# Output weights prepared from pair 48 on, first token rows ahead of the last transpose, and warming products on half the rows

## Chip, core and metric

The kernel runs on one core of one Trainium2 chip. The metric is the device time of one execution in microseconds (us). A core has TensorE (PE, the matrix engine; its weight loads are shown apart as PEld), VectorE (DVE), ScalarE (ACT), GpSimd (POOL) and SyncE (SP, which here issues nearly all DMAs). Each engine works through its own instructions in their order and waits for the others through semaphores. All DMAs that SP issues go through one queue to 16 DMA engines.

## The reference, cut to what matters

Two independent parts stand side by side in the output of 2048 x 1152.

Part A is attention with a compressive memory: 32 heads of 18, four segments of 512 tokens.

```python
q, k, v = x @ wq, x @ wk, x @ wv             # [2048, 576], 32 heads x 18
for s in range(4):                           # segments of 512 tokens
    p = softmax(q_s @ k_s.T * scale + causal mask)
    a_dot = p @ v_s
    a_mem = (phi(q_s) @ M) / (phi(q_s) @ z + 1e-6)
    o_s = g * a_mem + (1 - g) * a_dot
    M, z = M + phi(k_s).T @ v_s, z + sum(phi(k_s))
a = o @ wo                                   # the output product, [2048, 576]
```

Part B is a Fourier mixing by dense matrices: `y = Cr @ (x @ Hr.T) - Ci @ (x @ Hi.T)`, with Cr and Ci of 2048 x 2048 and Hr and Hi of 576 x 576.

## The kernel before

Products that need more than 16-bit accuracy are done with operands split in two, `hi` (rounded) and `lo` (the rest), as hi x lo + hi x hi + lo x hi. Rounding is done on ACT (`high`), the difference on DVE or POOL (`low`).

**Start.** `warm_up` (L237 to L239) issues products of a tile of ones while the first inputs are on their way; the tile of ones is set by DVE, nothing reads the result, and the first products of the projections (L250) follow on PE in its order. Projections, memory and lookups of the four segments fill the first 225 us or so.

**Pairs.** Attention then runs over 64 pairs of heads (a pair is two heads of a segment, one of them, `odd`, softmaxed row by row and then transposed by a DMA, the other, `even`, computed transposed at once). `attention()` is a software pipeline of 68 pairs `p`, each of eight slots; a slot is a stretch of recording that ends at a `yield`. Between slots the main loop records products of part B (`dense()`, L583, L628 to L633), as many as keep part B's planned cost in step with attention's. So the order of instructions on each engine is set when the program is recorded; it does not depend on times on the chip. Part B's left operands arrive in chunks (`craw`), four steps of a product to a chunk; ACT rounds them to `chi` (L451) and POOL, one tick later, makes `clo` (L456), two chunks ahead of their use. `later(n, ...)` puts a step n slots off.

**The tail of a pair's life.** In slot 5 `f_turn` asks SP for the transpose of the odd head's probabilities, from `hl` to `ptt` (L1003). `pv` (L1076, L1077) multiplies probabilities and values, `pv_out` normalises them, `turn_out` turns them and stores them to the DRAM buffers `od`.

**The output stage.** The output product works on token rows loaded back from `od`, two tiles of 128 tokens at a time (t and t + 8), by a scheme with seven products of half-size blocks instead of eight. It needs

- right operands: blocks of `wo` and sums and differences of them, each as hi and lo. `right_operands()` makes them; `load` fetches a row block of `wo` (`raw`), `first_block`, `second_row`, `tails`, `tail_difference` and `combined` round on ACT (`high`, L707), `difference` subtracts (L739), `block_low`, `row_low` and `combined_low` make low parts (`low`, L710) on POOL or DVE. Sums are written over `raw` in place. `combined` and `combined_low` write into the buffers of `qs0`/`ks0` to `qs2`/`ks2` when the last group of heads that uses them is done.
- left operands: `left(n)` is a generator of six steps that prepares tiles n and n + 8 from the rows `o_load` fetched. For n = 0 the rows go to `oraw` tiles in the buffers of `ks3`, `qs3`, `phi` and `plo`, and the results to those of `pf` and `hl`; for n = 0 all additions are on DVE, otherwise some are on POOL.

`PLAN` holds steps by slot: `at(p, slot, fn, ...)` runs `fn` right after that slot of pair p has been recorded. `right_operands` fills it. After the last pair the main loop records what is left of part B, with one step of `left(1)` for each piece, and then `output_stage()`, where `p1`, `p6`, `p5`, `p7`, `p2` follow each other for a tile pair; `p6` adds into `u` on DVE (L883), and `p7` writes the same PSUM tile next.

Before the change, the steps of `right_operands` stand at pairs 57 to 67: four `difference` and then four `combined_low` on DVE in pairs 64 and 65 for the first half, and eight more in pair 67 for the second, one after the other; rows 0 and 8 are asked for after slot 5 of pair 66, that is after the last transpose, rows 1 and 9 after slot 4 of pair 67, and all of `left(0)` is recorded at that place too.

Of the kernel before, what the change touches and what calls it, by code (L numbers as in the profile page):

```python
# [12 lines left out]
F32 = mybir.dt.float32  # L13
# [9 lines left out]
S, D, H, DH, NSEG, L = 2048, 576, 32, 18, 4, 512  # L23
P = 128
# [16 lines left out]
def infini_attention_and_fnet(ctx: ExitStack, tc: tile.TileContext, xT, wqk, w8, wv, wo, beta, xtT, cT, hT, out):  # L41
    nc = tc.nc
    act, dve, pool, pe = nc.scalar, nc.vector, nc.gpsimd, nc.tensor
# [23 lines left out]
    ones = const.tile([P, P], BF16, name="ones")  # L67
# [32 lines left out]
    ps = p1.enter_context(tc.tile_pool(name="ps1", bufs=2, space=PSUM))  # L100
# [43 lines left out]
    def wide_tile(cols):  # L144
        return lambda: wide.tile([P, cols], F32R, name="wide", tag="wide")
# [56 lines left out]
    for i in range(2):  # L202
        kn.append(tuple(sk.tile([P, D], F32R, name=f"kn{n}{i}") for n in "hl"))
        t = sk.tile([P, 2, H, 19], F32R, name=f"vn{i}")
# [3 lines left out]
    for i in range(3):  # L208
        t = sb.tile([P, H, 55], BF16, name=f"vs{i}")
# [25 lines left out]

    def warm_up():
        o = ps.tile([P, L], F32, name="warm", tag="acc", bufs=5)  # L237
        for _ in range(38):
            pe.matmul(o[:, :P], ones, ones, start=True, stop=True)  # L239

    def open_qk(s):
        ms = (0, 1, 2, 3) if s else (0, 1, 2, 3, 8)
        for m in ms:
            FIRST[m] = ps.tile([P, L], F32, name="qk", tag="acc", bufs=5)
        terms = {m: qk_terms(s, m) for m in ms}
        edges = (0, 6, 14) if s else (0, 1, 2, 3, 6, 9, 14)
        for a, b in zip(edges, edges[1:]):
            for m in ms:
                for n in range(a, b):
                    pe.matmul(FIRST[m], *terms[m][n], start=n == 0, stop=n == 13)  # L250
                if s and m == 0 and a:
                    accumulate(3, (1,))
            if s and a == 0:
                accumulate(3, (0,))
# [245 lines left out]
    for s in range(NSEG):  # L500
        more = s < 3
        if s == 0:
            warm_up()
# [55 lines left out]
    ps = ctx.enter_context(tc.tile_pool(name="ps2", bufs=2, space=PSUM, reuse_waits="tile"))  # L559
# [122 lines left out]
    O, LEFT, WO, TAIL = {}, {}, {}, {}  # L682
# [13 lines left out]
    def right_operands():  # L696
        raw, late = {}, {}

        def at(p, slot, fn, *a):
            PLAN.setdefault(8 * p + slot, []).append((fn, a))  # L700

        def load(k):
            raw[k] = wide.tile([P, D], F32, name="wide", tag="wide") if k == 3 else sb.tile([P, D], F32, name="raw", tag="raw", bufs=3)
            dma(raw[k], wo[k])

        def high(o, k, cs=slice(0, D)):
            act.activation(o, raw[k][:, cs], AF.Copy)  # L707

        def low(engine, o, hi, k, cs=slice(0, D), rows=slice(0, P)):
            engine.tensor_tensor(o[rows], raw[k][rows, cs], hi.bitcast(F32)[rows], OP.subtract)  # L710

        L_, R_ = slice(0, 288), slice(288, D)
        lower, upper = slice(0, 64), slice(64, P)

        def first_block(c):
            b = late["b", c] = wide.tile([P, 2, 288], F32R, name="wide", tag="wide")
            WO["B11", c] = b[:, 0], b[:, 1]
            high(b[:, 0], c, L_)

        def second_row(c):  # L720
            hi, lo = late["r", c] = [wide_tile(D)() for _ in range(2)]
            WO["B21", c], WO["B22", c] = ((hi[:, cs], lo[:, cs]) for cs in (L_, R_))
            high(hi, c + 2)

        def tails():
            w = late["w"] = [wide_tile(D)() for _ in range(2)]
            TAIL[1], TAIL[2] = ([t[:, cs] for t in w] for cs in (L_, R_))
            for t in w:
                high(t, 4)

        def tail_difference():
            d = wide.tile([P, 2, 288], F32R, name="wide", tag="wide")
            TAIL[0] = [d[:, i] for i in range(2)]
            for t in TAIL[0]:
                high(t, 4, L_)

        def difference(engine, o, a, b):
            (ko, co), (ka, ca), (kb, cb) = o, a, b
            engine.tensor_tensor(raw[ko][:, co], raw[ka][:, ca], raw[kb][:, cb], OP.subtract)  # L739

        def stage(i, n):
            return (sr if i < 2 else sq).tile([P, 4, 256], F32R, name="late", tag=f"{n}s{i}").rearrange("p a x -> p (a x)")

        def combined(c, n):
            k, names = ((c, ("T1", "T3")), (c + 2, ("T4", "T2")))[n]
            if c and n:
                hi, lo = ([t[:, D:D + 288] for t in late["s", i]] for i in (1, 0))
            else:
                late["s", 2 * c + n] = [stage(2 * c + n, x) for x in "qk"]
                hi, lo = ([t[:, L_], t[:, R_]] for t in late["s", 2 * c + n])  # L750
            for i, x in enumerate(names):
                WO[x, c] = hi[i], lo[i]
            if c and n:
                for i in range(2):
                    high(hi[i], k, (L_, R_)[i])
            else:
                high(late["s", 2 * c + n][0][:, :D], k)

        def combined_low(c, n, i):
            k, names = ((c, ("T1", "T3")), (c + 2, ("T4", "T2")))[n]  # L760
            low(dve, WO[names[i], c][1], WO[names[i], c][0], k, (L_, R_)[i])

        def block_low(c):
            low(pool, WO["B11", c][1], WO["B11", c][0], c, L_)

        def row_low(c):
            low(pool, late["r", c][1], late["r", c][0], c + 2)

        def sums(c):
            a, b = c, c + 2  # L770
            return (((a, L_), (a, R_), (a, L_)), ((a, R_), (b, R_), (a, R_)),
                    ((b, R_), (b, R_), (a, L_)), ((b, L_), (b, L_), (b, R_)))

        at(57, 2, load, 0)
        at(57, 4, load, 2)
        at(58, 2, first_block, 0)
        at(58, 2, second_row, 0)
        at(58, 2, load, 4)
        at(58, 4, load, 3)
        at(58, 4, block_low, 0)  # L780
        at(59, 4, row_low, 0)
        at(59, 2, tails)
        at(60, 4, lambda: low(pool, late["w"][0], late["w"][0], 4, rows=lower))
        at(61, 2, second_row, 1)
        at(61, 4, lambda: low(pool, late["w"][1], late["w"][1], 4, rows=upper))
        at(62, 4, difference, pool, (4, L_), (4, L_), (4, R_))
        at(63, 2, tail_difference)
        at(62, 6, row_low, 1)
        at(63, 4, lambda: low(pool, TAIL[0][0], TAIL[0][0], 4, L_, lower))
        at(63, 6, lambda: low(pool, TAIL[0][1], TAIL[0][1], 4, L_, upper))  # L790
        at(63, 6, load, 1)
        at(64, 2, first_block, 1)
        at(64, 4, block_low, 1)
        for i, x in enumerate(sums(0)):
            at(64, 3 + i, difference, dve, *x)
            at(65, 3 + i, combined_low, 0, i // 2, i % 2)
            at(67, 1, difference, dve, *sums(1)[i])
            at(67, 3, combined_low, 1, i // 2, i % 2)
        for n in range(2):
            at(65, 2, combined, 0, n)  # L800
            at(67, 2, combined, 1, n)
        for t in (0, 8):
            at(66, 5, o_load, t, lambda t=t: sq.tile([P, 4, 256], F32, name="oraw", tag="qs3" if t else "ks3").rearrange(
                "p a x -> p (a x)")[:, :5 * P].rearrange("p (k x) -> p k x", k=5))
        for t, tag in ((1, "phi"), (9, "plo")):
            at(67, 4, o_load, t, lambda tag=tag: sa.tile([P, 5, P], F32, name="oraw", tag=tag, bufs=2))
        at(67, 4, lambda: list(left(0)))

    def left(n):
        one, two = O.pop(n), O.pop(n + 8)  # L810
# [130 lines left out]
    sq = ctx.enter_context(tc.tile_pool(name="sb2q", bufs=1, side="right", reuse_waits="tile"))  # L941
    sa = ctx.enter_context(tc.tile_pool(name="sb2a", bufs=1, reuse_waits="tile"))
# [262 lines left out]
    while due:  # L1205
        tick()
    td = ta = 0.0
    right_operands()
    for n, w in enumerate(attention()):
        tick()  # L1210
# [3 lines left out]
        while td / total_d < ta / total_a:  # L1214
            t = next(d, BREAK)
# [5 lines left out]
    prepare = left(1)  # L1221
# [54 lines left out]
```

## Time and profile before

| | us |
|---|---|
| median of 3 runs | 993.38 (992.39 to 993.64) |
| profiled execution, time | 994.13 |
| profiled execution, span from first to last instruction | 992.4 |
| PE busy | 980.9 |
| DVE busy | 786.4 |
| ACT busy | 714.7 |
| POOL busy | 675.2 |

In the profile, times are in us unless marked ns. A row of a timeline gives start, duration, engine, line of the kernel, operation, output<-input with the program's names, shapes and count; what stands in brackets is the idle time before it and what ended it. SPq is SP's DMA queue issuing: its duration is that of the issue, not of the transfer. Matmuls are pipelined, so the duration of one is longer than its distance to the next. A row of windows gives from:to, its length, then for PE, PEld, DVE, ACT and POOL the busy time and number of instructions, the granted clock, the share of the DMA engines and the GB/s that they moved; where such a row is taken for the instructions of one line alone, it has only the engines that run that line.

### The profile page before, as it was taken

Reading aid. Unit: us, or ns where it says so; the run is one execution under the profiler, and the core shown is the slowest. Engines: PE = TensorE matmul, PEld = TensorE weight load, DVE = VectorE, ACT = ScalarE, POOL = GpSimd, SP = SyncE. Lnnn points to the kernel's source line nnn. Section 1 sums busy time; section 2 is a strip of 40 time slices with the busy share of each in tenths; the row PEclk is TensorE's granted clock in tenths of the full one; section 3 lists DMA queues with packets and bytes.
Section 4 is the critical chain, followed back from the end, with each engine's and each line's share of the span. In section 5 each row is a group of like instructions: output and inputs, shape, how many; then the busy total and the mean of one; then the engine's idle time right before and its main releaser. Section 6 shows DMA issues by size and latency. Waiting matters only on the chain.

```text
span 992.4 us, 25495 instructions
## 1 busy us (share of the span) xinstructions
PE 980.9 (99%) x9246; PEld 918.3 (93%) x9246; DVE 786.4 (79%) x2115; ACT 714.7 (72%) x1687; POOL 675.2 (68%) x744
## 2 busy tenths in 40 slices
PE   9999999999999999999999999999999999999998
PEld 8988989898999999999999999999999999999998
DVE  6657668584678787887898878888888898989985
ACT  6757576563888777877878788886777778788442
POOL 2657576686676667676775777767676667887561
PEclk9999999999999999999999999999999999999999
DMA  7537556777578898899999998779999999988663
GB/s 241 191 117 244 194 170 241 238 243 214 146 179 206 224 239 227 203 226 241 223 253 242 235 211 191 187 196 218 247 231 219 224 241 252 249 200 180 168 199 112
DMA packets 304351, 209.97 MB, mean 212 GB/s; under 512 B 204992, under 2 KB 259136, under 8 KB 304192
## 3 DMA queue, kind: packets, MB, share of 16 engines
q1 hardware_dynamic: 304000, 208.20, 80.9%
q8 instruction: 72, 1.18, 0.5%
q14 instruction: 55, 0.45, 0.1%
q10 hardware_dynamic: 224, 0.14, 0.0%
HBM read 122.37 MB, written 58.98 MB: 183 GB/s over the span
## 4 chain that ended last, share of the span: by engine, by line
PE 84%; DVE 7%; ACT 4%; DMA 2%; issue 2%; POOL 1%; SPq 0%; POOLq 0%; DVEq 0%; ACTq 0%
PE d L583 38%; PE s L958 7%; PE v L84 4%; PE pv L1076 4%; PE qk L250 4%; PE d L628 3%; PE d L629 3%; PE d L630 3%; PE t L861 2%; PE pv L1077 2%; PE m L363 1%; PE d L861 1%; PE s L861 1%; PE t L1032 1%; PE qk L84 1%
## 5 line engine op out<-in xcount | busy, mean ns | idle before, releaser
L964 DVE CUSTOM_DVE_ANT_0 s<-s,causal 128x128 f32<-128x128 f32 (+3 forms) x512 | 248.4, 503 | 94.2 <-PE s L958 85.0
L456 POOL TENSOR_TENSOR clo<-craw,chi 128x512 fp32r<-128x512 f32 x158 | 218.2, 1381 | 91.1 <-ACT chi L451 60.8
L583 PE MATMUL d<-wide,chi 128*128 128x288 f32 x1408 | 261.9, 303 | 0.2 <-DVE y L653 0.2
L583 PEld LDWEIGHTS d<-wide,chi 128*128 128x128 f32 x1408 | 210.6, 188 | 2.7 <-issue 0.7
L583 PE MATMUL d<-wide,clo 128*128 128x288 f32 x704 | 173.4, 313 | 0.0
L998 POOL TENSOR_TENSOR hl<-pf,hl 128x768 f16<-128x768 f32 x64 | 114.0, 1782 | 67.4 <-ACT hl L994 55.6
L958 PE MATMUL s<-ks,qs 108*128 108x128 bf16 (+3 forms) x512 | 132.9, 303 | 1.7 <-DVE negm L964 1.2
L1044 ACT ACTIVATE phi<-t 128x384 f16<-128x384 f32 x128 | 61.8, 483 | 100.1 <-PE t L1041 100.1
L987 ACT ACTIVATE pf<-s,nb 128x128 f32<-128x128 f32 (+3 forms) x256 | 128.3, 527 | 6.2
L583 PE MATMUL d<-ab,chi 128*128 128x288 f32 x640 | 123.3, 302 | 0.0
L1059 DVE TENSOR_TENSOR plo<-pf,phi 128x384 f16<-128x384 f32 (+1 forms) x128 | 122.3, 955 | 0.0
L583 PEld LDWEIGHTS d<-wide,clo 128*128 128x128 f32 x704 | 117.8, 189 | 1.4
L1045 ACT ACTIVATE pf<-t 128x384 f32<-128x384 f32 (+1 forms) x192 | 99.6, 519 | 6.6 <-PE t L1032 6.3
L451 ACT ACTIVATE chi<-craw 128x512 fp32r<-128x512 f32 x160 | 100.1, 626 | 4.0 <-DMA craw<-xtT 2.4
L583 PEld LDWEIGHTS d<-ab,chi 128*128 128x128 f32 x640 | 97.8, 188 | 0.5
L994 ACT ACTIVATE hl<-pf 128x768 f16<-128x768 f32 (+1 forms) x128 | 87.4, 729 | 2.0
L583 PE MATMUL d<-ab,clo 128*128 128x288 f32 x320 | 83.0, 308 | 0.0
L628 PE MATMUL d<-wide,chi 128*128 128x288 f32 x256 | 81.4, 318 | 0.0
L630 PE MATMUL d<-wide,clo 128*128 128x288 f32 x256 | 75.6, 296 | 0.9 <-POOL clo L456 0.9
L629 PE MATMUL d<-wide,chi 128*128 128x288 f32 x256 | 75.6, 295 | 0.0
L1059 POOL TENSOR_TENSOR plo<-pf,phi 128x384 f16<-128x384 f32 x64 | 61.7, 963 | 12.0 <-ACT pf L1045 9.1
L998 DVE TENSOR_TENSOR hl<-pf,hl 128x512 f16<-128x512 f32 x64 | 69.2, 1081 | 0.0
(285 smaller groups left out, 2521.9 us busy)
## 6 DMA issues: line engine op xcount, KB each, us to landing
craw<-cT SPq DMA_DIRECT2D x128, 256.0 KB
ks<-kd SPq DMA_DIRECT2D x32, 432.0 KB
qs<-qd SPq DMA_DIRECT2D x32, 432.0 KB
craw<-xtT SPq DMA_DIRECT2D x32, 320.0 KB
vd<-vs SPq DMA_DIRECT2D x16, 440.0 KB
vst<-vd SPq DMA_DIRECT2D x32, 220.0 KB
qd<-p SPq DMA_DIRECT2D x16, 384.0 KB
kd<-p SPq DMA_DIRECT2D x16, 384.0 KB
```

What stands on the lines that cost most here:

```text
L451: act.activation(hi, raw[:, :4], AF.Copy)
L456: engine.tensor_tensor(lo, raw[:, :4], hi.bitcast(F32), OP.subtract)
L583: pe.matmul(o[h], a, b[:, h * 288:h * 288 + 288], start=start, stop=stop)
L628: pe.matmul(o, xh[:, k], wl[k][:, cs], start=k == 0, stop=False)
L629: pe.matmul(o, xh[:, k], wh[k][:, cs], start=False, stop=False)
L630: pe.matmul(o, xl[:, k], wh[k][:, cs], start=False, stop=False)
L958: pe.matmul(o[:, c:c + w], q[:, i * P:w], k[:, :w], start=True, stop=True)
L964: dve.tensor_tensor_reduce(o[:, c:c + w], o[:, c:c + w], CAUSAL[0][:, L - w:], scale=scale, scalar=-LOWEST, op0=OP.add, op1=OP.min, accum_ ...
L987: act.activation(f[:, FIRST_COL[i]:FIRST_COL[i] + w], o[:, c:c + w], AF.Exp, bias=nb[:, i:i + 1], scale=-1.0)
L998: engine.tensor_tensor(hl[:, 1, a:b], f[:, a:b], hl[:, 0, a:b], OP.subtract)
L1045: act.activation(f[:, r:r + w], o[:, :w], AF.Exp, bias=LIFT, scale=SCALE)
L1059: (pool if kind == 2 else dve).tensor_tensor(lo[:, a:b], f[:, a:b], hi[:, a:b], OP.subtract)
```

## The change

Three edits, all in the order of recording; the products and their operands stay the same.

1. The steps of `right_operands` move from pairs 57 to 67 to pairs 48 to 66, and stand one to a slot: DVE's steps only after slots 2 and 5. The `difference` steps come in pairs 58, 59, 61 and 62, the `combined_low` steps in pairs 62, 64, 65 and 66 (two each). In the last two pairs `left(0)` is recorded in six pieces, after slots 1 to 6 of pair 67, not in one piece after slot 4.
2. The four `o_load` of tiles 0, 8, 1 and 9 all come after slot 4 of pair 66, ahead of the last `f_turn` in slot 5.
3. `warm_up` issues 34 products on all rows, one on the lower 64 rows after each of the products 20 to 25, and eight pairs of products, lower and upper 64 rows (into two PSUM tiles), after product 29.

```diff
     def warm_up():
         o = ps.tile([P, L], F32, name="warm", tag="acc", bufs=5)
-        for _ in range(38):
+        u = ps.tile([P, L], F32, name="warm", tag="acc", bufs=5)
+        lower, upper = slice(0, 64), slice(64, P)
+        for n in range(34):
             pe.matmul(o[:, :P], ones, ones, start=True, stop=True)
+            if 20 <= n < 26:
+                pe.matmul(o[:, :P], ones[lower], ones[lower], start=True, stop=True)
+            if n == 29:
+                for _ in range(8):
+                    pe.matmul(o[:, :P], ones[lower], ones[lower], start=True, stop=True)
+                    pe.matmul(u[:, :P], ones[upper], ones[upper], start=True, stop=True)
...
-        at(57, 2, load, 0)
-        at(57, 4, load, 2)
-        at(58, 2, first_block, 0)
...
-        at(63, 6, load, 1)
-        at(64, 2, first_block, 1)
-        at(64, 4, block_low, 1)
-        for i, x in enumerate(sums(0)):
-            at(64, 3 + i, difference, dve, *x)
-            at(65, 3 + i, combined_low, 0, i // 2, i % 2)
-            at(67, 1, difference, dve, *sums(1)[i])
-            at(67, 3, combined_low, 1, i // 2, i % 2)
-        for n in range(2):
-            at(65, 2, combined, 0, n)
-            at(67, 2, combined, 1, n)
+        at(48, 2, load, 0)
+        at(48, 4, load, 2)
+        at(49, 2, load, 4)
+        at(49, 4, load, 3)
+        at(50, 2, first_block, 0)
...
+        at(58, 6, load, 1)
+        at(60, 2, first_block, 1)
+        at(60, 4, block_low, 1)
+        for c in range(2):
+            for i, x in enumerate(sums(c)):
+                at(58 + 3 * c + i // 2, (2, 5)[i % 2], difference, dve, *x)
+        for p, c, n in ((61, 0, 0), (63, 0, 1), (64, 1, 1), (65, 1, 0)):
+            at(p, 2, combined, c, n)
+            for i in range(2):
+                at(p + 1, (2, 5)[i], combined_low, c, n, i)
         for t in (0, 8):
-            at(66, 5, o_load, t, lambda t=t: sq.tile(... tag="qs3" if t else "ks3") ...)
+            at(66, 4, o_load, t, lambda t=t: sq.tile(... tag="qs3" if t else "ks3") ...)
         for t, tag in ((1, "phi"), (9, "plo")):
-            at(67, 4, o_load, t, lambda tag=tag: sa.tile([P, 5, P], F32, name="oraw", tag=tag, bufs=2))
-        at(67, 4, lambda: list(left(0)))
+            at(66, 4, o_load, t, lambda tag=tag: sa.tile([P, 5, P], F32, name="oraw", tag=tag, bufs=2))
+        prepare = []
+        at(67, 1, lambda: prepare.append(left(0)))
+        for n in range(6):
+            at(67, 1 + n, lambda: next(prepare[0]))
```

More of the change, by code (lines that the diff above doesn't have):

```diff
@@ L772, in sums @@
                     ((b, R_), (b, R_), (a, L_)), ((b, L_), (b, L_), (b, R_)))
-        at(57, 2, load, 0)
-        at(57, 4, load, 2)
-        at(58, 2, first_block, 0)
[L777 to L790, printed above, removed]
-        at(63, 6, load, 1)
-        at(64, 2, first_block, 1)
-        at(64, 4, block_low, 1)
-        for i, x in enumerate(sums(0)):
-            at(64, 3 + i, difference, dve, *x)
-            at(65, 3 + i, combined_low, 0, i // 2, i % 2)
-            at(67, 1, difference, dve, *sums(1)[i])
-            at(67, 3, combined_low, 1, i // 2, i % 2)
@@ L799, in right_operands @@
-        for n in range(2):
-            at(65, 2, combined, 0, n)
-            at(67, 2, combined, 1, n)
+        at(48, 2, load, 0)
[3 more added lines that the diff above has]
+        at(50, 2, first_block, 0)
+        at(51, 2, second_row, 0)
+        at(51, 4, block_low, 0)
+        at(52, 4, row_low, 0)
+        at(52, 2, tails)
+        at(53, 4, lambda: low(pool, late["w"][0], late["w"][0], 4, rows=lower))
+        at(53, 2, second_row, 1)
+        at(54, 4, lambda: low(pool, late["w"][1], late["w"][1], 4, rows=upper))
@@ new lines, in right_operands @@
+        at(55, 4, row_low, 1)
+        at(56, 4, difference, pool, (4, L_), (4, L_), (4, R_))
+        at(57, 2, tail_difference)
+        at(57, 4, lambda: low(pool, TAIL[0][0], TAIL[0][0], 4, L_, lower))
+        at(58, 4, lambda: low(pool, TAIL[0][1], TAIL[0][1], 4, L_, upper))
+        at(58, 6, load, 1)
[4 more added lines that the diff above has]
+                at(58 + 3 * c + i // 2, (2, 5)[i % 2], difference, dve, *x)
@@ L802, in right_operands @@
+        for p, c, n in ((61, 0, 0), (63, 0, 1), (64, 1, 1), (65, 1, 0)):
+            at(p, 2, combined, c, n)
+            for i in range(2):
+                at(p + 1, (2, 5)[i], combined_low, c, n, i)
         for t in (0, 8):
-            at(66, 5, o_load, t, lambda t=t: sq.tile([P, 4, 256], F32, name="oraw", tag="qs3" if t else "ks3").rearrange(
+            at(66, 4, o_load, t, lambda t=t: sq.tile([P, 4, 256], F32, name="oraw", tag="qs3" if t else "ks3").rearrange(
                 "p a x -> p (a x)")[:, :5 * P].rearrange("p (k x) -> p k x", k=5))
```

## The prediction

> **What bounds the kernel now.** I read the page first, then who TensorE (PE) waited for over the whole run, then the tail of the run by windows, by the chain that ended last and by each engine's timeline.
>
> ```profile
> span 992.4 us, 25495 instructions
> PE 980.9 (99%) x9246; PEld 918.3 (93%) x9246; DVE 786.4 (79%) x2115; ACT 714.7 (72%) x1687; POOL 675.2 (68%) x744
> ...
> PE t L861 <- DVE u L883: 1.9, 1, 1.9
> PE pv L1077 <- DVE plo L1059: 0.4, 1, 0.4
> PE d L583 <- DVE y L653: 0.2, 1, 0.2
> ```
>
> PE is busy 980.9 of 992.4 us, and the change takes no product of the computation from it. So all that preparation moved off the tail can win is PE's waits near the tail: three of them, 1.9, 0.4 and 0.2 us (columns: total, times, longest), all ended by VectorE (DVE). That is 2.5 us, 0.25% of the run.
>
> ```profile
> 860.00:880.00 20.00, 19.96 (x220) 18.66 (x216) 18.03 (x53) 14.84 (x33) 15.68 (x18) 1.00 0.85 202
> 900.00:910.00 10.00, 9.42 (x101) 8.75 (x98) 9.79 (x24) 7.86 (x18) 7.57 (x7) 1.00 0.95 214
> 910.00:920.00 10.00, 10.00 (x113) 9.71 (x113) 9.86 (x20) 8.60 (x20) 7.43 (x7) 1.00 0.54 128
> 930.00:940.00 10.00, 8.09 (x62) 7.84 (x61) 9.67 (x22) 3.67 (x10) 5.50 (x7) 1.00 0.47 124
> ...
> 922.15 4.64 DMA oraw<-od
> 926.82 1.28 DVE ls L829
> ...
> 936.95 0.38 DVE u L883
> 937.38 1.32 PE t L861 x8
> ```
>
> The windows give, per stretch, busy time of PE, weight loads, DVE, ScalarE (ACT), GpSimd (POOL). DVE goes from 90% (18.03 of 20) to 98% in 900 to 920 and 97% in 930 to 940; there PE loses 0.58 us (9.42 of 10) and 1.91 us (8.09 of 10). The chain says how the big one comes about: the token rows (oraw) land, `left(0)` starts on DVE at 926.82, and DVE works in one piece until u (L883) lets PE go on at 937.38.
>
> **The weights moved off DVE's tail.**
>
> ```profile
> 923.13 0.45 DVE L739 TENSOR_TENSOR raw<-raw 128x288 f32<-128x288 f32 x1
> ...
> 925.72 0.82 DVE L710 TENSOR_TENSOR late<-wide,late 128x288 fp32r<-128x288 f32 x2
> 926.82 1.28 DVE L829 TENSOR_TENSOR ls<-oraw 128x256 f32<-128x256 f32 x1 [0.28 <-DMA oraw<-od]
> ...
> 929.29 0.41 DVE L837 TENSOR_TENSOR lb<-oraw,lb 128x256 fp32r<-128x256 f32 x1
> ...
> 931.82 1.12 DVE L849 TENSOR_TENSOR l<-ls,l 128x512 fp32r<-128x512 f32 x1
> ...
> 936.88 0.45 DVE L883 TENSOR_TENSOR u<-t,u 128x288 f32<-128x288 f32 x1
> ```
>
> In pair 67 four sums and four low parts hold DVE from 923.13 to 926.54, then it waits 0.28 us for oraw: 3.69 us ahead of `left(0)`. All eight go to pairs 61 to 66. With them gone, u hangs on `left(0)` and `left(1)`, which stand between, and PE's 1.91 us are won if these begin or run 1.91 us earlier.
>
> That they do not get all 3.69 us comes of the second edit. The four oraw requests now stand ahead of the last transpose on SP's queue, in pair 66, and the first waits there for the last read of ks3 (L1041).
>
> ```profile
> 917.44 0.27 PE L1041 MATMUL t<-qs,ks 111*128 111x256 bf16 x1
> 918.43 3.04 SPq L1003 DMA_TRANSPOSE ptt<-hl  x1
> 921.57 1.13 SPq L687 DMA_DIRECT2D oraw<-od  x2
> 916.00:919.00 3.00, 3.00 (x41) 2.93 (x40) 3.00 (x6) 2.17 (x6) 3.00 (x4) 1.00 0.00 0
> 920.00:923.00 3.00, 3.00 (x40) 3.00 (x40) 2.66 (x7) 0.00 (x0) 2.66 (x4) 1.00 1.11 208
> 927.00:932.00 5.00, 5.00 (x56) 4.93 (x55) 4.84 (x10) 3.19 (x9) 2.58 (x3) 1.00 1.17 302
> oraw<-od SPq DMA_DIRECT2D x4, 320.0 KB
> ```
>
> Before, the DMA engines stood idle from 916 to 919 (0 GB/s, last column), the transpose of 20 blocks of 128x128 f16 (0.66 MB) ran at 208 GB/s and was through near 923, and oraw followed. Now the first request can go at 917.75 and starts to move about 1.2 us later, as the transpose did (issue 918.43, idle to 919). Four times 320 KB is 1.31 MB, at 302 GB/s 4.3 us: through at 923.3. SP issues the transpose behind them at 917.75 + 4 x 0.57 = 920.0, but its data come after theirs in the queue: 923.3 + 0.66 MB at 208 GB/s (3.2 us) = 926.5, landed near 926.9, 3.5 us later than before. Earliest 923.4, if the queue lets it pass; latest 928.5, if SP's 3.04 us of issue start only when the rows are through. I take 926.9. Who waits for it:
>
> ```profile
> 928.05 0.20 PE L1076 MATMUL pv<-vst,ptt 128*128 128x55 bf16 x1
> ...
> 929.73 0.69 PE L583 MATMUL d<-ab,chi 128*128 128x288 f32 x4
> 930.26 0.43 PE L583 MATMUL d<-ab,clo 128*128 128x288 f32 x2
> ...
> 925.77 0.62 ACT L451 ACTIVATE chi<-craw 128x512 fp32r<-128x512 f32 x1
> ...
> 926.88 0.42 ACT L834 ACTIVATE lb<-oraw 128x256 fp32r<-128x256 f32 x1
> ...
> 926.52 1.30 POOL L456 TENSOR_TENSOR clo<-craw,chi 128x512 fp32r<-128x512 f32 x1 [3.86 <-DMA od<-ogt]
> ```
>
> First PE, with the last pv out of ptt at 928.05: 1.15 us to spare. Second ACT: lb lies in the buffer from which the transpose reads (hl), so L834 waits on ACT until 926.9, and in the built order the last chi now stands behind it instead of ahead of it. It ends at 926.9 + 0.42 + 0.62 = 927.9, and clo on POOL at 929.3. The last chunk is steps 12 to 15 of the product; ab tiles are its right operands from step 11 on, and the rows at 929.73 and 930.26 are step 12's, the second with ab: it asks for chi and clo 1.8 and 1.0 us later than they are there. No stall, but not far from one. Third DVE: the low part of lb waits for ACT. `left(0)` begins at 923.2 instead of 926.82, has its first four operations done by 925.7 (2.5 us to 929.29 before), stands until lb's high part is there at 927.3, and needs 3.65 us for the rest (929.29 to 932.94): 931.0 instead of 932.9. A few tenths can go, as s1 on ACT comes behind chi. I count -1.8; the ends are -1.91, all of the wait, and -0.3, with the transpose at 928.5.
>
> **The same weights put into pairs 58 to 66.**
>
> ```profile
> L1003 SPq DMA_TRANSPOSE ptt<-hl x64: 3037/3745/6270, 258.7 to 918.4; - x64
> ...
> 895.00:905.00 10.00, 2.92 (x4) 0.00 (x0) 1.00 0.94 185
> ...
> 905.00:915.00 10.00, 4.11 (x4) 0.00 (x0) 1.00 0.98 223
> ```
>
> One transpose a pair, 63 pairs from 258.7 to 918.4: 10.5 us a pair, of which DVE has 1.0 free (18.03 of 20). The last two rows are DVE's sums (L739) and low parts (L710) in pairs 64 and 65 by themselves: eight took 7.0 us, 0.88 each, where row 923.13 has 0.45 for one; they cost PE the 0.4 + 0.2 us. Now there are two a pair in 58, 59, 61, 64, 65 and 66 and four in 62, at 0.45 to 0.88 each 0.9 to 1.8 us a pair, twice that in 62. I take 0.45 of the 0.6 us as won; bounds: all 0.6, or 0.6 lost once more. The five loads of 288 KB (1.0 us each at 302 GB/s) stand ahead of the transposes of pairs 48, 49 and 58 instead of 57, 58 and 63, where no PE wait came of them; ACT's and POOL's shares of them have 25% and 20% of their engines free (14.84 and 15.68 of 20). Nothing for these; bounds -0.1 and +0.4.
>
> **The warming products.** 38 become 34, with six on 64 rows among them and eight pairs, lower and upper half: 56 in all.
>
> ```profile
> 1.13 4.24 PE L239 MATMUL warm<-ones 128*128 128x128 bf16 x38 [1.13 <-DVE ones L68]
> 5.13 2.06 PE L250 MATMUL qk<-xh,wide 128*128 128x512 f32 x4
> ...
> 7.30 1.09 PE L250 MATMUL qk<-xl,wide 128*128 128x512 f32 x4
> L239 PE MATMUL warm<-ones x38: 289/314/314, 1.1 to 5.1; 128*128 128x128 bf16 x38
> 44.44 0.50 PE L84 MATMUL v<-wide,xh 128*128 128x288 f32 x2
> ```
>
> 38 in 4.0 us is 0.107 us each. Four real products take 2.06 us before and 1.09 after about 7.1 us: the array's clock is at half until then. If a pair runs side by side there are 48 turns, and the first real product comes 1.07 us later; one after another, 56 turns and 1.9 us later. If the clock comes at 7.1 us as before, real work lost in the slow stretch counts half: 0.53 to 0.95 us, less about 0.1, as the first four no longer wait for their weights. Taken: +0.6; ends 0 (the clock comes earlier) and +2.9 (below). The Trainium skill (TensorE: Matmul & The Clock Gate, Part 3) has products on different row groups start within 4 ns of each other, which would be the 48 turns; no row here shows it.
>
> **Sum:** -1.8 - 0.45 + 0.6 = -1.65 us. The profiled execution took 994.13 us (span 992.4), 0.75 over the median of 993.38; against it 992.5, against the median 991.7.
>
> **Rivals.**
> *The last transpose comes too late.* If it lands at 928.5 or after, pv waits 0.5 us or more on PE, chi and clo follow as late, and DVE resumes `left(0)` 1.6 us later, so that most of the 1.9 us stays. For it: the queue is served in order, and SP's issue alone is 3.04 us. Against: 1.15 us of room. It would come to -0.3 - 0.45 + 0.6 + 0.5 = +0.3: 993.7.
> *The array empties at each change between whole and half rows.* A product holds the array 0.314 us from start to end but follows the last after 0.107; if that overlap is lost at each of 14 changes, 2.9 us are added to 1.07, the real work starts near 9.1, and it costs 1.0 + 2.0 = 3.0 us: 994.1. Against it stands a change to 64 columns and back, after which two products take 0.50 us where such pairs take 0.43: 0.07 a change, 1 us in all. The Trainium skill (TensorEngine Tiling, Key Properties) says that changing the tiling mode drains TensorE; that speaks against this edit, and the row above agrees only in small.
> *DVE's backlog reaches PE: slower.* The 16 moved operations at 0.88 us are 14.1 us in nine pairs that have 9.3 free. If PE has no cover, 4.8 us come back as waits of s, pv and d for DVE: -1.8 + 0.6 + 4.8 = +3.6: 997.0. It decides from where the backlog exceeds what pairs 64 and 65 bore (about 5 us for 0.6 lost); the spread is wider now, which speaks against it.
> *The clock comes a window earlier,* with a PE more densely fed: the four slow products go back to 1.09 us, and the edit wins 0.4 to 1 instead of losing 0.6: 990.4. Nothing before the 20th product changes, so little speaks for it.
>
> **How the numbers follow.** Forecast 0.50 (own range 990.9 to 992.6), late transpose 0.20, drain 0.10, backlog 0.10, early clock 0.10. The range 990.4 to 994.2 leaves out the backlog and half of the early clock. A measurement of this kernel tells 0.2% (2 us) from no change, so faster means under 991.4: the early clock and half of the forecast, 0.34. Slower is over 995.4: the backlog, and a few hundredths of the drain and of a late transpose together, 0.14.
>
> **What would show it.** Right: no PE wait for DVE u, `left(0)`'s first operation some 3.5 us earlier, a DVE wait in it that ACT or the transpose ends, real products from about 6.2 us on. Wrong: PE waits for ptt or chi near the end of attention, for DVE in pairs 58 to 66, or a first real product past 7 us.

## The result: 0.9% slower, and the profile after

| | before | after |
|---|---|---|
| median, us | 993.51 (992.39 to 993.99, 4 runs) | 1002.29 (1000.61 to 1004.27, 4 runs) |
| ratio to before | | 1.0091, 95% interval 1.0068 to 1.0114 |
| span of the profiled execution, us | 992.4 | 1001.6 |

The forecast was 991.7 within 990.4 to 994.2. First the head of the page and the waits of PE, as shown of before:

```profile
span 1001.6 us, 25527 instructions
PE 987.0 (99%) x9264; PEld 922.2 (92%) x9264; DVE 785.7 (78%) x2115; ACT 714.2 (71%) x1687; POOL 672.5 (67%) x744
```

```profile
PE d L591 <- DVE y L661: 1.8, 1, 1.8
PE t L871 <- DVE u L893: 1.7, 1, 1.7
PE s L968 <- DVE nd L415: 1.6, 1, 1.6
PE s L968 <- DVE negm L974: 1.2, 2, 0.8
PE pv L1086 <- DMA ptt<-hl: 1.2, 1, 1.2
```

Of the 9.2 us, PE is busy 6.1 longer (987.0 for 980.9), though its real work is the same (more warming products, and stretches at half clock, below), and stands 3.1 longer. The wait for u that the edit was to remove is still there, 1.7 for 1.9 us; the wait for y has grown from 0.2 to 1.8 us, and that for ptt is new. (Lines behind the warm-up are 8, later 10, higher than before.)

**Where it builds up.** The same product of each pair can be found in both traces; its distance from the first warming product tells how far the changed kernel lies behind. It is 2.7 us at the first real product, 1.8 at the first pair (waits in the projections before it give 0.9 back), still 1.5 to 1.8 up to pair 53, 3.2 at pair 61, 6.7 at pair 63, 5.7 from pair 65 up to the wait for ptt, and 8.7 at the last product. Four places, then: the start, pairs 53 to 61, pair 62, and the tail.

**The start**, by PE's timeline:

```profile
1.13 2.42 PE L241 MATMUL warm<-ones 128*128 128x128 bf16 x21 [1.13 <-DVE ones L68]
3.49 0.28 PE L243 MATMUL warm<-ones 64*128 64x128 bf16 x1
3.70 0.29 PE L241 MATMUL warm<-ones 128*128 128x128 bf16 x1
3.93 0.29 PE L243 MATMUL warm<-ones 64*128 64x128 bf16 x1
...
5.90 0.61 PE L241 MATMUL warm<-ones 128*128 128x128 bf16 x4
...
7.78 2.06 PE L258 MATMUL qk<-xh,wide 128*128 128x512 f32 x4
...
9.97 1.08 PE L258 MATMUL qk<-xl,wide 128*128 128x512 f32 x4
```

Alternating whole and half products start 0.21 to 0.23 us apart instead of 0.107: each change of rows costs 0.1 us. Real products begin at 7.78 instead of 5.13, and the first four still take 2.06 us: the clock rises at about 9.8, not at 7.1.

**Pair 62**, by DVE's timeline and then PE's:

```profile
880.93 0.88 DVE L747 TENSOR_TENSOR wide<-wide,raw 128x288 f32<-128x288 f32 x1
881.73 0.46 DVE L718 TENSOR_TENSOR late<-raw,late 128x288 fp32r<-128x288 f32 x1
...
884.43 1.09 DVE L747 TENSOR_TENSOR wide<-wide 128x288 f32<-128x288 f32 x1
885.45 0.45 DVE L718 TENSOR_TENSOR late<-raw,late 128x288 fp32r<-128x288 f32 x1
...
886.16 1.60 DVE L1069 TENSOR_TENSOR plo<-pf,phi 128x384 f16<-128x384 f32 x1
...
889.34 0.45 DVE L661 TENSOR_TENSOR y<-y,d 128x288 f32<-128x288 f32 x1
```

```profile
889.84 0.53 PE L591 MATMUL d<-wide,chi 128*128 128x288 f32 x2 [1.78 <-DVE y L661]
```

Two differences and two low parts, 2.9 us, stand ahead of the step that empties PE's bank into y, and PE waits 1.78 us. That is half of what this pair lost. The other half is the clock, by windows of 3.41 us around this wait and around the one for u (the third number from the end is the granted clock):

```profile
887.07:890.48 3.41, 1.63 (x13) 1.40 (x11) 3.27 (x8) 3.41 (x7) 2.50 (x3) 1.00 0.80 248
890.48:893.90 3.42, 3.42 (x34) 3.12 (x33) 3.08 (x10) 0.29 (x1) 0.00 (x0) 0.50 0.52 163
941.68:945.10 3.42, 1.69 (x13) 1.45 (x12) 3.35 (x10) 0.33 (x2) 0.49 (x1) 1.00 0.22 86
945.10:948.51 3.41, 3.41 (x16) 3.41 (x16) 2.75 (x8) 0.15 (x1) 2.09 (x4) 0.50 0.00 0
```

Behind each of the two waits the clock is 0.50 for one stretch of 3.41 us, in which up to 1.7 us of work are lost. Not every run has these stretches: one of the four, with a mean clock of 1.000, took 1001.2 us. So 7.7 of the 8.8 us can come without them.

**The tail**, by the timelines of SP's queue, ACT, DVE and PE:

```profile
923.40 2.08 SPq L695 DMA_DIRECT2D oraw<-od  x4
925.59 7.43 SPq L1013 DMA_TRANSPOSE ptt<-hl  x1
```

```profile
935.08 0.42 ACT L844 ACTIVATE lb<-oraw 128x256 fp32r<-128x256 f32 x1 [7.70 <-DMA ptt<-hl]
935.41 0.62 ACT L459 ACTIVATE chi<-craw 128x512 fp32r<-128x512 f32 x1
```

```profile
928.69 0.41 DVE L839 TENSOR_TENSOR ls<-oraw 128x256 f32<-128x256 f32 x1
...
935.53 0.43 DVE L847 TENSOR_TENSOR lb<-oraw,lb 128x256 fp32r<-128x256 f32 x1 [5.16 <-ACT lb L844]
...
944.04 0.44 DVE L893 TENSOR_TENSOR u<-t,u 128x288 f32<-128x288 f32 x1
```

```profile
935.03 0.20 PE L1086 MATMUL pv<-vst,ptt 128*128 128x55 bf16 x1 [1.16 <-DMA ptt<-hl]
```

The last transpose, issued behind the rows, takes 7.43 us to issue (3.04 before) and comes at 935. PE waits for it 1.16 us; ACT has stood 7.70 us with lb, whose buffer that transpose reads, and DVE 5.16 us behind ACT. What DVE had gained it gave back there, and u is as late as before.

### The profile page after: what moved, and what is told of

It is laid out like the page before. It is cut to its first block, busy times and chain, and to the rows that moved or that the text cites. A ratio compares the mean times of both kernels' runs of the same rounds, so it can differ in the third digit from the quotient of the medians.

```text
span 1001.6 us, 25527 instructions
## 1 busy us (share of the span) xinstructions
PE 987.0 (99%) x9264; PEld 922.2 (92%) x9264; DVE 785.7 (78%) x2115; ACT 714.2 (71%) x1687; POOL 672.5 (67%) x744
## 4 chain that ended last, share of the span: by engine, by line
PE 81%; DVE 6%; ACT 3%; POOL 3%; DMA 3%; issue 2%; SPq 1%; POOLq 0%; DVEq 0%; ACTq 0%
PE d L591 35%; PE s L968 7%; PE v L84 4%; PE qk L258 4%; PE pv L1086 4%; PE d L638 3%; PE d L636 3%; PE d L637 3%; PE t L871 2%; PE pv L1087 2%; PE s L871 1%; PE m L371 1%; PE d L871 1%; PE t L1042 1%; PE qk L84 1%
```

## The experiments

Three theories of the loss were to be told apart. Theory 1: three edits, each with a cost of its own. Theory 2: one cause, DVE's moved steps, from which all else follows. Theory 3: the late stretches at half clock hang on the phase that the start gives the clock, and not on the waits.

**One edit at a time**

`e1_warm_only`: the kernel before with the new `warm_up`.

> The kernel before with the new warm-up alone. Theory 1 (three separate costs: warm-up, weights, rows): the products on half the rows take longer than the whole ones they replace, the first real product starts at about 7.8 us instead of 5.1, the matrix engine stays 1.8 us behind to the end, and the run is 1.8 us longer (1.3 to 2.3). Theory 2 (one cause, VectorE's preparation steps, everything else follows from it): a shift at the start is taken up by the waits at the start of attention (2.2 us of them before), and the run is within 0.6 us of the kernel before. Theory 3 (the two stretches of half clock late in the changed kernel hang on the phase that the start gives the clock, not on waits): a stretch of half clock late in this run too, 1.7 us on top.

Measured: 997.53 (996.82 to 998.05), ratio 1.0042 (1.0027 to 1.0057). That is more than theories 1 and 2 had, and the late half clock of theory 3 is not in the trace. First real product again at 7.78, and here the clock came at 12.0:

```profile
7.78 2.06 PE L258 MATMUL qk<-xh,wide 128*128 128x512 f32 x4
...
10.06 1.91 PE L258 MATMUL qk<-xl,wide 128*128 128x512 f32 x4
...
12.12 1.09 PE L258 MATMUL qk<-xh,wide 128*128 128x512 f32 x4
```

So the warm-up alone, priced at +0.6, is nearly half of the loss. The wait for u of 1.9 us is as before, without a half clock behind it.

`e2_rows_only`: the kernel before with the four row requests in slot 4 of pair 66.

```diff
-            at(66, 5, o_load, t, ...
+            at(66, 4, o_load, t, ...
-            at(67, 4, o_load, t, ...
+            at(66, 4, o_load, t, ...
```

> The kernel before with the four requests for token rows ahead of the last transpose, and nothing else. Theory 1: the last transpose lands late behind the rows, the matrix engine waits about 1 us for ptt, the wait for u stays at 1.5 to 2.5 us, and the run is 1 to 3.5 us longer, the upper end if a stretch of half clock follows. Theory 2: in the changed kernel the transpose was late because VectorE was; alone this edit costs nothing and may win a little as the rows land earlier: -0.8 to +0.3 us.

Measured: 993.26 (992.14 to 994.53), ratio 0.9994 (0.9985 to 1.0003). A wait for ptt of 0.4 us comes, the wait for u shrinks from 1.9 to 1.2. By itself this edit costs nothing, as theory 2 had it for this run.

`e3_weights_only`: the kernel before with the new places of the weights, and `left(0)` in six pieces.

> The kernel before with the weights prepared from pair 48 on and the first left operands in six pieces; rows and warm-up as before. Theory 1: the wait for y in pair 62 comes back (about 1.8 us) and with it a stretch of half clock (1.7 us), some 0.5 to 1 us more in pairs 53 to 60; at the end the wait for u (1.9 us) is gone or short: +1 to +3 us in all. Theory 2: all of the loss is here: +6 to +9 us. Theory 3: waits as in theory 1, but no half clock, since the start is that of the kernel before: 0 to +1 us.

Measured: 995.34 (993.86 to 997.33), ratio 1.0019 (1.0008 to 1.0030). The wait for y of 1.8 us is there, the wait for u 1.2 us.

`e4_weights_thin62`: the same, with the low parts of pair 62 in pair 63.

```diff
-                at(p + 1, (2, 5)[i], combined_low, c, n, i)
+                at(p + 1 + (p == 61), (2, 5)[i], combined_low, c, n, i)
```

> The run before this one, with the two low parts of pair 62 put into pair 63, so that no pair has more than two of VectorE's steps. If the four steps in one pair are what breaks (theory 1), the wait for y in pair 62 and the half clock go, and the run is 1 to 2.5 us shorter than the kernel before. If it is the amount of work in pairs 58 to 66 (rival), the wait only moves to pair 64 or 65 and the run is within 1 us of the weights-only one.

Measured: 993.91 (993.32 to 994.6), ratio 1.0004 (0.9994 to 1.0013). The wait for y is gone, that for u is 0.7. The time is not the 1 to 2.5 us under the kernel before that was expected. What stays: pair 54 loses 1.0, pairs 59 to 63 lose 1.5 against the kernel before. Theory 2 falls with e1, theory 1 is short: the parts' medians add to +4.1 - 0.2 + 1.9 = +5.8, and the whole is +8.8.

**The warm-up taken apart, and the parts together**

`f1_pairs_only`: 34 whole products and the eight pairs in one block, no alternation (the diff is against the new `warm_up`).

```diff
-            if 20 <= n < 26:
-                pe.matmul(o[:, :P], ones[lower], ones[lower], start=True, stop=True)
```

> The kernel before with the new warm-up but without its six single products on half the rows: 34 whole products and, in one block, the eight pairs on lower and upper rows. The new warm-up alone gave 1.0042: first real product at 7.78 us instead of 5.13, full clock at 12.01 instead of 7.15. Theory A (the cost is in the changes between whole and half rows, about 0.1 us each, 14 of them): here 2 changes and 42 turns of 0.107, first real product near 5.8 us, full clock no later than 7.2, time +0.4 to +0.7, 993.9 to 994.2. Theory B (products on half the rows don't count for the clock, in whatever order): first real product near 5.8 as well, but full clock at 9 us or later, two to three us of real products at half speed more, time +1.7 to +2.7, 995.2 to 996.2.

Measured: 994.34 (992.53 to 997.85), ratio 1.0010 (0.9998 to 1.0023). First real product at 5.78, and the clock record has full speed at 7.1. Theory A holds; products on half the rows do count when they run in pairs side by side.

`f2_whole63`: `for _ in range(63)` in the warm-up of before.

> The kernel before with 63 whole warming products instead of 38, so that the first real product comes about as late as with the new warm-up (1.13 + 63 x 0.107 = 7.87 us), but with no product on half the rows. Theory B (half-row products don't count for the clock) and theory A (the changes cost) both expect full clock by about 7.2 us, the last warming products at double speed, no real product at half speed, and a loss of 2.4 less the 1.0 that the slow stretch cost before: +1.4, 994.9. Rival C (a later start by itself makes the clock late, since the clock waits for real products): full clock at 9.8 to 12 us and +3 to +4, 996.5 to 997.5, as with the new warm-up.

Measured: 998.19 (995.8 to 999.73), ratio 1.0044 (1.0029 to 1.0059): by its time rival C, by its trace not. Full speed came at 5.5 us and the four first real products took 1.17 us; the loss at the first of them was 1.55 us, as A and B had it. The rest came later: a wait of 3.4 us for DVE (w, L415) near 222 us, and two half-clock stretches, behind it and behind the wait for u. The one run without such a stretch (mean clock 1.000) took 995.8. Why that wait grew was not traced.

`f3_after_old_warm`: the changed kernel with the 38 whole products.

> The changed kernel with the 38 whole warming products of before: weights from pair 48 on and the rows ahead of the last transpose. If the parts add, weights alone (+1.9) and rows alone (-0.2) give +1.7: 995.2, with a wait for y of 1.8 us in pair 62 and a wait for u of at most 1.2. If the two meet in the tail (the first part's lb and chi stand behind the late transpose on ScalarE, and left(0) on VectorE behind lb): ptt wait over 1 us and u wait 1.7 again, +3 to +3.5, 996.5 to 997. If the half clock after the waits hangs on the late start of the clock, there is none here; if it hangs on the waits, one or two stretches of 3.4 us show and it is 998 or more.

Measured: 997.25 (995.67 to 1000.45), ratio 1.0035 (1.0021 to 1.0049), twice the sum of its parts (+1.7). By their mean clock, five of the ten runs had a stretch at half clock (0.998 or less, median 999.4) and five none (0.999 or more, median 995.9). The two edits meet in the tail: the wait for u is 1.7 us again, with 1.2 in each part alone, and ptt costs 0.9. One half-clock stretch stands behind the wait for y; the clock had come at 4.7, so it does not need the late start.

`f4_after_thin62`: the whole change, with the edit of e4.

> The whole changed kernel, but the two low parts that stood in pair 62 beside two differences go one pair later. If the four steps of pair 62 make y late, and the half clock of 3.4 us behind it follows from that wait: both go, 1.78 + 1.7 less, 998.8. If the half clock comes anyway at that place of its 3.413 us grid: only the wait goes, 1000.5. If the backlog merely moves to pair 63: a wait of the same size for y, d or s one pair later, and 1002.3 again.

Measured: 999.54 (999.01 to 1001.6), ratio 1.0055 (1.0038 to 1.0073), 3.6 us less by the ratios. The wait for y and the half clock behind it go together. The wait for u (1.7) stays, but it falls into two windows of the clock (below) and no half clock follows it in this trace.

**Alternation alone, the buffer alone, and two mended versions**

`g1_singles_only`: 34 whole products with the six single ones on half the rows, no pairs.

> The kernel before with 34 whole warming products and the six single ones on the lower 64 rows between the 21st and the 27th, without the eight pairs. If the alternation is what delays start and clock: the twelve changes take 0.1 us each, first real product at about 6.8 us, and the stretch of alternating products (3.5 to 5.9 us) doesn't count towards the clock, which comes between 9 and 12.5 us: +2.5 to +4, 996 to 997.5. If it is the later start by itself (as 63 whole products gave first real at 6.68 but the clock at 5.46 us): clock before 7.5 and +0.8 to +1.2, 994.5.

Measured: 995.77 (995.0 to 1001.21), ratio 1.0024 (1.0010 to 1.0038), less than expected, but start and clock are as the alternation has them:

```profile
6.70 2.06 PE L253 MATMUL qk<-xh,wide 128*128 128x512 f32 x4
8.55 0.63 PE L253 MATMUL qk<-xh,w8h 128*128 128x512 f32 x1
8.98 1.13 PE L253 MATMUL qk<-xl,wide 128*128 128x512 f32 x4
```

First real product at 6.70, full speed at 9.05. f2, with its first real product at 6.68, had it at 5.5: it is the alternation that delays the clock, not the later start.

`g2_after_lb_apart`: the whole change, lb in tiles of its own (the diff is against the changed kernel).

```diff
-            b = sa.tile([P, 6, P], F32R, name="lb", tag="hl", bufs=2)
-            a22, tl = b[:, :4], b[:, 4:]
+            a22, tl = (wide.tile([P, 4, P], F32R, name="wide", tag="wide") for _ in range(2))
+            tl = tl[:, :2]
```

> The whole changed kernel, but lb (A22 and the two tails of the first part) lies in two tiles of its own and no longer in the buffer that the last transpose reads. If the wait for u of 1.73 us comes of ScalarE and VectorE standing behind that buffer: no idle of 5 us before L839's successors, the wait for u under 0.5 us, no half clock near 945, chi and clo earlier: 2 to 3.4 us less than the changed kernel, 999 to 1000.3; the wait for ptt of 1.2 us stays. If VectorE's own queue holds u back: the same wait for u and 1002.3.

Measured: 999.75 (999.03 to 1000.42), ratio 1.0059 (1.0045 to 1.0072), 3.2 us less by the ratios. ACT, then DVE, then PE's waits:

```profile
929.14 0.42 ACT L844 ACTIVATE wide<-oraw 128x256 fp32r<-128x256 f32 x1 [0.43 <-DMA oraw<-od]
929.47 0.62 ACT L459 ACTIVATE chi<-craw 128x512 fp32r<-128x512 f32 x1
```

```profile
932.41 0.41 DVE L846 TENSOR_TENSOR ls<-ls,oraw 128x256 f32<-128x256 f32 x1
932.74 0.41 DVE L847 TENSOR_TENSOR wide<-oraw,wide 128x256 fp32r<-128x256 f32 x1
```

```profile
PE d L591 <- DVE y L661: 1.8, 1, 1.8
...
PE t L871 <- DVE u L893: 0.7, 1, 0.7
```

DVE goes through `left(0)` without the 5.16 us pause, and the wait for u falls from 1.7 to 0.7. The wait for ptt, expected to stay, is gone: PE was 1.3 us later at pair 65 in this execution and reached the same product at 935.05.

`g3_rows_lb_sums66`: before, with e2's and g2's edits and the four differences of the second column in pair 66.

```diff
-            at(67, 1, difference, dve, *sums(1)[i])
-            at(67, 3, combined_low, 1, i // 2, i % 2)
+            at(66, (2, 3, 5, 6)[i], difference, dve, *sums(1)[i])
+            at(67, 2, combined_low, 1, i // 2, i % 2)
...
-            at(67, 2, combined, 1, n)
+            at(67, 1, combined, 1, n)
...
```

> The kernel before with its warm-up and its weights, but the first token rows ahead of the last transpose, lb in tiles of its own, and only the four differences of the second column of weights moved, from pair 67 to pair 66. If VectorE's tail is what makes u late, 1.9 us of it go ahead: the wait for u falls under 0.5 us, and with it the half clock of 3.4 us that some runs of the kernel before show behind that wait; a wait for ptt of 0.4 us comes. 991.3 to 992.3. If the four differences delay pair 66's own work on VectorE: waits for negm or plo of 1 us, and 993.5 or more.

Measured: 994.16 (993.29 to 997.51), ratio 1.0007 (0.9997 to 1.0017). The rival came: there is a new wait for plo of 1.4 us, and the wait for u is 1.2, as with the rows alone (e2). So four steps at once in pair 66 make PE wait as they did in pair 62.

`g4_change_mended`: the change with the old warm-up, e4's and g2's edits, and the two low parts of the tails in pair 54 (the diff, against the changed kernel, shows these alone).

```diff
...
-        at(53, 4, lambda: low(pool, late["w"][0], ...
+        at(54, 2, lambda: low(pool, late["w"][0], ...
-        at(54, 4, lambda: low(pool, late["w"][1], ...
+        at(54, 6, lambda: low(pool, late["w"][1], ...
...
```

> The change with what went wrong taken out: 38 whole warming products, the two low parts of pair 62 in pair 63, lb in tiles of its own, and GpSimd's two low parts of the tails in pair 54 instead of 53 and 54. If the causes named are all: no wait for y and for u over 0.5 us, no half clock, no loss at pair 54; the 1.3 us that pairs 59 to 63 lost with the weights alone stay: 992.5 to 993.5. If the loss at pair 54 only moves, 993.5 to 994.5. If something not named costs still more, over 995.

Measured: 993.22 (992.25 to 993.72), ratio 0.9993 (0.9984 to 1.0002), beside 993.89 for the kernel before in the same batch.

```profile
PE s L960 <- DVE negm L966: 1.6, 3, 0.8
...
PE pv L1079 <- DVE plo L1061: 0.7, 2, 0.4
PE pv L1078 <- DMA ptt<-hl: 0.6, 1, 0.6
```

No wait for y or u is left, and no half clock in any of its 11 runs, by their mean clock of 0.999 to 1.000. Taking out the causes named returns 9.7 us by the ratios, all of the loss. The loss of pair 54 only moved, to pair 55 (0.9). A gain over before is not shown: the interval reaches over 1.

## Why the prediction was wrong

Each of the three signs that were to show it wrong came: a wait for ptt, a wait for DVE in pairs 58 to 66, and a first real product past 7 us. The steps, one by one:

**Warming products: the term was +0.6, it is +4.1 alone (e1).** Two things failed. The prediction counted 48 turns at 0.107 us, with at most 0.07 us for a change; a change costs 0.1, and the first real product was at 7.78, not 6.2. And "if the clock comes at 7.1 us as before" was false: it came at 9.8, 12.0, 10.9 and 12.0 in four traces with this warm-up, against 4.3 to 7.2 in the nine with whole products or pairs, of which before's 7.15 was the latest. The rival of the changes between whole and half rows, at 0.10, had the mechanism and nearly the size (+3.0), and its rule from the Trainium skill (TensorEngine Tiling, Key Properties) was the one to believe: g1 and f1 show that the alternation does it. From the end of the alternation at 5.9 us, the clock took 3.1 to 6.1 us in the four traces and g1, as it takes 3.1 to 6.0 us from PE's start at 1.13 without it. So it came as if the time up to 5.9 had not counted. The Trainium skill (TensorE: Matmul & The Clock Gate, Part 1) has full clock after one busy window of about 3.4 us that runs freely; these spreads, one window wide, agree.

**Weights in pairs 58 to 66: the term was -0.45, it is +1.9 alone (e3).** "Four in 62" stood in the text, but they were spread as an average over the pair: what matters is how many steps stand in a row ahead of a step that PE waits for. e4, which takes two of the four away, recovers 1.4 us. "Nothing" for POOL's parts was wrong too. DVE's plo of pair 53 before, then POOL after, where the low part (L718) has pushed clo and hl beside plo, then DVE after:

```profile
791.40 0.68 DVE L1059 TENSOR_TENSOR plo<-pf,phi 128x512 f16<-128x512 f32 x1
```

```profile
789.99 1.42 POOL L718 TENSOR_TENSOR wide<-raw,wide 64x576 fp32r<-64x576 f32 x1
...
792.58 1.28 POOL L464 TENSOR_TENSOR clo<-craw,chi 128x512 fp32r<-128x512 f32 x1
793.82 1.66 POOL L1008 TENSOR_TENSOR hl<-pf,hl 128x768 f16<-128x768 f32 x1
```

```profile
793.41 2.62 DVE L1069 TENSOR_TENSOR plo<-pf,phi 128x512 f16<-128x512 f32 x1
```

It takes 2.62 us instead of 0.68, and PE waits 0.82 for negm behind it. POOL's two operations end at 793.86 and 795.48, plo at 796.03: it ends 0.55 us after the second, as if it had only begun then. The Trainium skill (SBUF — State Buffer, SBUF: two separate sides) has VectorE and GpSimd share a pair of ports as a lock that one of them holds for a whole instruction; these rows agree. The trace of before bears it out: 34 of DVE's 64 plo of this size begin with over 0.1 us of a POOL instruction still to run, and each of them ends 0.54 to 0.57 us behind the end of that POOL instruction. What is new is a second POOL instruction right behind the first: the six traces with the low parts at their new place (after, e3, e4, f3, f4, g2) have one plo of 2.6 us each, the others none over 2.2. In g4 the loss came back one pair later in the same way. POOL's low part (797.44 to 798.87) makes DVE's first plo of that pair 1.73 us long, where it took 0.56 before; the second then begins 0.02 us behind POOL's hl, where before it began 0.41 us ahead of it:

```profile
800.84 1.67 POOL L1000 TENSOR_TENSOR hl<-pf,hl 128x768 f16<-128x768 f32 x1 [0.41 <-ACT hl L996]
```

```profile
800.86 2.19 DVE L1061 TENSOR_TENSOR plo<-pf,phi 128x512 f16<-128x512 f32 x1
```

The further loss in pairs 59 to 63 (1.5 us in e4) was not traced.

**The tail: the term was -1.8, and the wait for u went from 1.9 to 1.7.** Right was when `left(0)` begins: 928.69, where 923.2 plus the lag of 5.7 is 928.9. The buffer chain was seen too ("lb lies in the buffer from which the transpose reads"), but not its date: the transpose landed at 935.0, against 926.9 forecast. Of the 8.1 us, 5.7 are the lag of the whole kernel by then; the rest goes beyond the "latest 928.5", since SP's issue took 7.43 us and not 3.04. The 3.04 was the mis-sized price in it: it is the shortest of the 64 issues in the row that the prediction shows (3037/3745/6270 ns), taken where the DMA engines had stood idle. In e2, where nothing else was changed, the issue took 5.21 and PE waited 0.4. So "no stall, but not far from one" was a stall, and the rival of the late transpose, at 0.20, was the right mechanism. g2 shows that the buffer, and not DVE's own queue, held u for 1.0 of its 1.7 us. What makes the issue longer was not separated.

**What had no term at all: the half clock.** A wait of 1.8 us was priced at 1.8; each of the two cost up to 1.7 more. What matters, as far as the traces go, is how much of a wait lies in one window of 3.413 us, on a grid counted from where the trace's clock first rose: every fall and rise of the clock lies whole windows from there. First before, whose wait for u of 1.91 us cost no clock, then e3, whose wait for y was 1.8 but fell into two windows:

```profile
935.57:938.99 3.42, 1.61 (x12) 1.62 (x13) 3.28 (x10) 0.00 (x0) 0.00 (x0) 1.00 0.24 91
938.99:942.40 3.41, 3.41 (x28) 3.41 (x28) 3.38 (x7) 2.61 (x8) 3.05 (x5) 1.00 0.11 38
```

```profile
883.28:886.69 3.41, 2.11 (x18) 1.69 (x16) 3.27 (x9) 2.96 (x7) 2.64 (x2) 1.00 0.97 298
886.69:890.11 3.42, 2.92 (x38) 2.78 (x39) 3.38 (x11) 1.42 (x3) 0.86 (x2) 1.00 0.34 123
```

In the traces of this case, windows with 1.7 us of idle or less kept the clock, all with 1.9 or more lost it, and between 1.73 and 1.81 both occurred (before's 1.8 kept it, f3's 1.8 did not). f4 and g1 fit too: their waits for u of 1.7 and 1.9 us fell into two windows, with at most 1.04 and 1.14 us in one, and cost no clock. Half a window is 1.71. The wait for u of before is at this edge, and its runs differ: of 71 timed ones with their clock on record, 39 have a mean clock of 0.998 or less and a median of 994.3, 32 have 0.999 or more and 993.1. The mean does not tell where in a run the clock fell, so that the wait for u does it there is likely, not shown.

**Theory 3** has this much: the phase decides on which side a wait of 1.8 us falls; the late start is not needed (f3). The sum of the parts (+5.8) and the whole (+8.8) differ by the 1.7 that f3 lies above its two parts and by 1.3 beyond. The 1.7 is the tail and the half clock together, as f3's two groups of runs show; the 1.3 is no more than one stretch at half clock, and was not separated.

## What to carry to other kernels

Count a moved step by what stands right behind it on its engine, not by the engine's mean load: two more steps in pair 62 made PE wait 1.8 us at 90% load; with the two in the next pair that wait did not come. Where a buffer is reused, date the last reader by the queue that serves it, and give the first writer another buffer before anything in that queue is moved. And price a PE wait of about 1.7 us or more at up to twice its length, since the clock may fall behind it.

## What the runs showed of the hardware that was not expected

- A single wait with 1.73 to 1.91 us of idle in one window of 3.413 us can bring a stretch at half clock; the six that did brought one window each. The Trainium skill (TensorE: Matmul & The Clock Gate, HAM oscillation) advises against idle gaps of over about 3.4 us; here half of that was enough, so the measurement decides.
- Single products that alternate between 128 and 64 rows cost 0.1 us a change at half clock, and the clock rose as late as if they had not been work (g1); lower and upper halves in pairs start within 0.01 us of each other, at about 0.107 us a pair, and the clock rose as with whole products (f1).
- A subtraction on DVE (plo, 128x512) that begins beside a POOL instruction ends 0.54 to 0.57 us behind the end of that one, or of the next if it follows at once. Alone it takes 0.68 us, so up to 2.6.
- Behind four row requests, the issue of the last DMA transpose took 5.2 to 7.4 us in seven traces, against 3.0 in the seven without them there. Elsewhere in the kernel before it takes up to 6.3 us, so the requests need not be the only reason.
